# A delta-rule attention with a two-layer network behind it: 17 wide weight parts, a first inverse on blocks of 16, 64-column key products, beta in one load

## The chip, the core and the metric

The program runs on one core of a Trainium2 chip. A core has TensorE (PE, matrix products into PSUM), VectorE (DVE), ScalarE (ACT), GpSimd (POOL), and SyncE (SP), which here issues all DMAs. Each engine has its own stream of instructions and waits on semaphores. The metric is device microseconds of one execution, lower is better; the time before is the median of three runs.

## What is computed

For 4 x 8 heads of 768 tokens and 48 dimensions a state S (48 x 48) is carried along the tokens; its reads y, all heads side by side, are the rows of a two-layer network with relu squared.

```python
k_n = k / (np.linalg.norm(k, axis=-1, keepdims=True) + 1e-06)
for t in range(S):
    kt, vt, bt = (k_n[:, :, t], v[:, :, t], beta[:, :, t, None])
    y[:, :, t] = np.einsum('bhd,bhde->bhe', q[:, :, t], state)
    v_old = np.einsum('bhde,bhd->bhe', state, kt)
    state = state + bt[..., None] * np.einsum('bhd,bhe->bhde', kt, vt - v_old)
x = y.transpose(0, 2, 1, 3).reshape(B * S, H * D)      # 3072 x 384
out = np.maximum(x @ w_in, 0.0) ** 2 @ w_out           # 384 x 2048, 2048 x 384
```

q, k, v and beta are float32, the two weight matrices are float64.

## The kernel before

**Tiling.** The 768 tokens are 12 units of 64 (C); two units are a pair. Within a unit the recurrence is a triangular system: with L the strictly lower part of the scaled k k^T, T is the inverse of I + L, and w = T (v - k S). L is cut into 32 x 32 blocks (HB). All heads go through DVE at once: partitions hold the head and a row, the free dimension holds columns.

**What a unit needs.** `load_blocks` brings k or q as 32 x 32 blocks into one of two staging buffers kb, 8 DMAs on SP each, and `turned` (L246) transposes them with one DVE instruction into kt or qt; the first ones go through TensorE (`turned_by_pe`, L240, copied by ACT in L243). `load_v` and `load_rows` bring v and a second copy of k (kpad).
- `key_products`, once per pair: 32 x 32 products of kt with itself, for each of 32 heads and two units two diagonal blocks (L266) and one low block (L270), 192 in all; ACT copies the low part to mt.
- `prepare`: norms and beta (bt, 16 DMAs a pair in `load_beta`), lt = scaled L.
- `invert`: 31 steps of two DVE operations on all 32 x 32 blocks of the pair (L312 a product into tmp, L314 a subtraction from z). `ended` scales z and turns it twice (L319, L322 zt, L324 t).
- `below`, per unit: the off-diagonal block of T by two passes of products (L332, L333, then L343, L344) with ACT copies into tt.
- `query_products`: q k^T (L357), masked by DVE into ap (L361).
- `state_part`: k S (L387), subtracted from vt by DVE (L389); q S (L396), T times the rest (L402), copied to w; the state (L412) and y (L418).

**The network, `moe(u)`.** TensorE turns y (L431, three transposes for each of two token halves); ACT and DVE split it into a high and a low fp32r half, x_h (L433) and x_l (L434). For eight column pairs: up products L464 (three terms by three row parts, twice: 18 products), relu (L471), square (L472), cast h_h (L474) on ACT, the low half h_l (L443) on DVE, later 12 down products L451 into two PSUM tiles o. L486 copies the result, L491 writes it.

**The weights** come in 28 parts (128 x 512 of w_in, 128 x 384 of w_out) as pairs of 32-bit words. `split_weights` makes two fp32r halves of each part: `least` (Abs on ACT L125, a maximum on POOL L126), `words` (DVE L133, L136, L139, L140; a cast on ACT L143), `low` (three products on TensorE L149, a copy on ACT L150). Parts use two rooms (tiles a and rest; r and h_l) up to part 10 and one room after it.

**Order.** TensorE, SP, DVE and ACT run in the order in which the code is written (`tc.manual_schedule`); POOL's is left to a scheduler. `weave` lays generators against the 34 steps of `moe(u - 1)`, each step at a position in the stage, given in fractions:

```python
parts.append((loads(u), [0.02, 0.2, 0.3, 0.57, 0.62, 0.78, 0.85, 0.96], True))
parts.append((key_products(nxt), [0.18], False))           # odd u
parts.append((inverse, spread(0.34, 1, F1), True))         # odd u, F1 = 21
parts.append((inverse, spread(0, 0.26, HB - 1 - F1), True))  # even u
parts.append((splits, spread(0, 0.88, NW - 6), False))     # u = 1
```

A stage u is thus the attention of unit u with the network of unit u - 1. Odd stages hold the key products of the next pair, its preparation and 21 inversion steps; even stages the other ten, `ended`, and `below` for both units. Before stage 1 stands the start: unit 0's attention, with the first weight parts split between. Where a generator asks for a weight that isn't split, `half_of` drives the split on at that place.

Of the kernel before, what the change touches and what calls it, by code (L numbers as in the profile page):

```python
# [20 lines left out]
def kernel(  # L21
# [13 lines left out]

    nc = tc.nc
    B, H, S, D = q.shape
    DM, DF = w_in.shape
    P = 128
    C = 64  # L40
    HB = 32
    NP = H // 2
# [4 lines left out]
    units = S // C  # L47

    turn = [0, 0]
    const = ctx.enter_context(tc.tile_pool(name="const", bufs=1))  # L50
    wpool = ctx.enter_context(tc.tile_pool(name="weights", bufs=1))
    apool = ctx.enter_context(tc.tile_pool(name="attn", bufs=2))
# [5 lines left out]

    warm = const.tile([P, 1], F32, name="warm")
# [3 lines left out]
    kb = []  # L63
    for i in range(2):
        t = const.tile([P, 2 * X, C], F32, name=f"kb{i}")
        nc.gpsimd.memset(t[:, :, D:], 0.0)
        kb.append(t)
    plus, minus = [const.tile([P, P], F32R, name=n) for n in ("plus", "minus")]
    eye = spool.tile([P, 512], F32, name="a")[:, :P]
    make_identity(nc, eye)  # L70
    nc.scalar.copy(out=plus, in_=eye)
    nc.scalar.mul(out=minus, in_=eye, mul=-1.0)
    ident = plus.bitcast(F32)

    mask = const.tile([P, C], F32, name="mask")
    nc.gpsimd.memset(mask, 1.0)
    for b in range(2):
        half = mask[b * C:(b + 1) * C]
        nc.gpsimd.affine_select(out=half, in_=half, pattern=[[1, C]], base=0, channel_multiplier=-1,
                                compare_op=ALU.is_gt, fill=0.0)  # L80
    kp = const.tile([P, 2, X, C], F32, name="kpad")
    nc.gpsimd.memset(kp[:, :, :, D:], 0.0)
    ttile = []
    for i in range(2):
        tt = const.tile([P, 2, X, C], F32, name=f"tt{i}")
        nc.gpsimd.memset(tt[:, :, :, :HB], 0.0)
        ttile.append(tt)
# [3 lines left out]
    PC = 512  # L91
    EACH = PC // P
    weight_parts = []
    for part in range(DF // PC):
        weight_parts += [("wi", (kt, part), w_in[kt * P:(kt + 1) * P, part * PC:(part + 1) * PC]) for kt in range(KT)]
        weight_parts += [("wo", ft, w_out[ft * P:(ft + 1) * P]) for ft in range(part * EACH, (part + 1) * EACH)]
    NW = len(weight_parts)
    place = [f"w{x}" for x in range(NW)]
    raws = []
    halves = {}  # L100

    rooms = [(spool, "a", "rest"), (mpool, "r", "h_l")]
    AHEAD = 10

    def fetch(n):
        for _ in range(n):
            x = len(raws)
            if x < NW:
                src = weight_parts[x][2]
                raw = wpool.tile([P, src.shape[1], 2], I32, name=place[x])  # L110
                nc.sync.dma_start(out=raw.rearrange("p a b -> p (a b)"), in_=src.bitcast(I32))
                raws.append(raw)

    def room(x, n):
        pool, first, second = rooms[x % 2 if x < AHEAD else 0]
        return pool.tile([P, PC], I32, name=first)[:, :n], pool.tile([P, PC], I32, name=second)[:, :n]

    def split_weights():


        def least(x):

            w1 = raws[x][:, :, 1]
            a, rest = room(x, w1.shape[1])
            nc.scalar.activation(out=a.bitcast(F32), in_=w1.bitcast(F32), func=AF.Abs)  # L125
            nc.gpsimd.tensor_scalar(out=a.bitcast(F32), in0=a.bitcast(F32), scalar1=LEAST, scalar2=None, op0=ALU.max)  # L126
            return x, a, rest

        def words(x, a, rest):
            raw = raws[x]  # L130
            w1 = raw[:, :, 1]

            nc.vector.tensor_scalar(out=a, in0=a, scalar1=3, scalar2=0x3FFFFFF8,  # L133
                                    op0=ALU.logical_shift_left, op1=ALU.bitwise_and)

            nc.vector.scalar_tensor_tensor(out=a, in0=w1, scalar=-0x40000000, in1=a,  # L136
                                           op0=ALU.bitwise_and, op1=ALU.bitwise_or)

            nc.vector.tensor_scalar(out=w1, in0=a, scalar1=-0x800000, scalar2=None, op0=ALU.bitwise_and)  # L139
            nc.vector.scalar_tensor_tensor(out=rest.bitcast(F32R), in0=raw[:, :, 0].bitcast(U32), scalar=2.0 ** -52,  # L140
                                           in1=w1.bitcast(F32), op0=ALU.mult, op1=ALU.mult)
            hl = wpool.tile([P, 2, raw.shape[1]], F32R, name=place[x])
            nc.scalar.copy(out=hl[:, 0], in_=a.bitcast(F32))  # L143
            return x, a, rest, hl

        def low(x, a, rest, hl, bank):
            ps = bank()[:, :hl.shape[2]]
            for n, (m, y) in enumerate(((ident, a.bitcast(F32)), (minus, hl[:, 0]), (plus, rest.bitcast(F32R)))):
                nc.tensor.matmul(ps, lhsT=m, rhs=y, start=(n == 0), stop=(n == 2))  # L149
# [508 lines left out]
```

## Time and profile before

| | us |
|---|---|
| median of three runs | 794.68 (790.76 to 798.01) |
| the profiled execution, own time | 788.97 |
| its span in the profile | 787.3 |
| TensorE busy | 644.2 (82%) |
| VectorE busy | 381.9 (49%) |
| ScalarE busy | 313.0 (40%) |
| GpSimd busy | 53.8 (7%) |
| weights landed | about 62 |

The profiled execution lies 0.7% under the median. A row of the profile names a line, an engine, an operation, the tile written and the tiles read; "<-" in brackets behind it names what ended the wait ahead of it. A product of f32 operands shows as two TensorE records, so 64 such products are 128 records. The granted clock is a share of TensorE's full speed. Shares over the whole span mix the start, stage 1 and the later stages, which the prediction takes apart.

### The profile page before, as it was taken

What the parts mean: (1) busy time and instruction counts of PE and PEld (TensorE: products, weight loads), DVE (VectorE), ACT (ScalarE), POOL (GpSimd) and SP (SyncE); (2) the same over time, 40 slices, a digit from 0 to 9 for tenths busy, and PEclk for the clock granted to TensorE, in tenths of its full rate; (3) what the DMA queues carried; (4) which work ended last, traced back from release to release, by engine and by line L of the source; (5) the groups of instructions that cost most, each with busy time, mean ns of one, the idle gap of its engine ahead of it and who ended that gap; (6) DMA issues with size and microseconds to landing.
All of it is one profiled execution on the core that took longest, in us unless ns stands there. A gap on an engine that the chain in (4) does not pass through costs nothing.

```text
span 787.3 us, 25119 instructions
## 1 busy us (share of the span) xinstructions
PE 644.2 (82%) x11368; PEld 592.5 (75%) x11368; DVE 381.9 (49%) x777; ACT 313.0 (40%) x544; POOL 53.8 (7%) x55
## 2 busy tenths in 40 slices
PE   4407757575788979979979889798898998899997
PEld 3304635363587979979979879798798998799997
DVE  0597533645484225871337833178623577232121
ACT  2215533343334524334533445243544343445443
POOL 2203111222101000001000010000100000000000
PEclk9999777987898988998989989899999899899999
DMA  7993200010132311313212323114132023110000
GB/s 144 191 397 100 38 2 2 1 21 0 22 41 43 59 28 22 50 15 62 42 24 43 41 44 62 23 22 62 25 55 49 4 50 53 22 24 22 1 20 21
DMA packets 152939, 38.30 MB, mean 49 GB/s; under 512 B 146176, under 2 KB 149248, under 8 KB 152832
## 3 DMA queue, kind: packets, MB, share of 16 engines
q1 hardware_dynamic: 152832, 36.69, 23.3%
q8 instruction: 89, 1.46, 0.8%
q14 instruction: 18, 0.15, 0.1%
HBM read 31.95 MB, written 4.72 MB: 47 GB/s over the span
## 4 chain that ended last, share of the span: by engine, by line
PE 65%; DVE 18%; issue 6%; ACT 3%; SPq 2%; DMA 2%; POOL 1%; DVEq 0%; POOLq 0%
PE h L464 25%; PE o L451 23%; DVE tmp L312 3%; DVE z L314 3%; PE g L149 2%; PE g L266 2%; PE g L387 2%; PE g L357 2%; PE g L402 1%; DVE zt L322 1%; PE g L412 1%; PE g L418 1%; DVE h_l L443 1%; DVE rest L140 1%; PE g L396 1%
## 5 line engine op out<-in xcount | busy, mean ns | idle before, releaser
L451 PE MATMUL o<-w,h_h 128*128 128x384 f32 x768 | 209.2, 354 | 0.0
L464 PE MATMUL h<-x_h,w 128*128 128x256 f32 x1152 | 186.4, 300 | 24.3 <-DVE x_l L434 12.6
L443 DVE TENSOR_TENSOR h_l<-r,h_h 128x512 fp32r<-128x512 f32 x96 | 66.0, 688 | 258.1 <-PE o L451 163.2
L464 PEld LDWEIGHTS h<-x_h,w 128*128 128x128 f32 x1152 | 166.6, 204 | 29.7 <-issue 15.4
L451 PEld LDWEIGHTS o<-w,h_h 128*128 128x128 f32 x768 | 139.8, 197 | 2.4
L451 PE MATMUL o<-w,h_l 128*128 128x384 f32 x384 | 133.5, 348 | 0.0
L471 ACT ACTIVATE r<-h 128x512 f32<-128x512 f32 x96 | 57.4, 598 | 177.9 <-PE h L464 173.0
L464 PE MATMUL h<-x_l,w 128*128 128x256 f32 x576 | 105.8, 295 | 0.3
L464 PEld LDWEIGHTS h<-x_l,w 128*128 128x128 f32 x576 | 88.1, 203 | 0.9 <-DVE x_l L434 0.9
L451 PEld LDWEIGHTS o<-w,h_l 128*128 128x128 f32 x384 | 75.5, 197 | 0.0
L314 DVE TENSOR_TENSOR z<-z,tmp 128x31 f32<-128x31 f32 (+15 forms) x186 | 64.0, 344 | 6.4
L312 DVE TENSOR_TENSOR tmp<-lt,z 128x31 f32<-128x31 f32 (+15 forms) x186 | 62.6, 337 | 4.2 <-DVE lt L302 0.5
L472 ACT ACTIVATE r<-r 128x512 f32<-128x512 f32 x96 | 60.7, 632 | 3.1
L474 ACT CAST h_h<-r 128x512 fp32r<-128x512 f32 x96 | 59.6, 621 | 3.0
L143 ACT CAST w<-a 128x384 fp32r<-128x384 f32 (+1 forms) x23 | 12.7, 553 | 86.8 <-DVE rest L140 86.8
L149 PE MATMUL g<-a,plus 128*128 128x384 f32 (+1 forms) x42 | 24.6, 674 | 21.5 <-ACT w L150 16.2
L266 PE MATMUL g<-kt 48*32 48x32 f32 x1536 | 25.8, 225 | 15.3 <-issue 15.3
L126 POOL TENSOR_SCALAR a<-a 128x384 f32<-128x384 f32 (+1 forms) x23 | 29.7, 1292 | 112.9 <-ACT a L125 89.0
L266 PEld LDWEIGHTS g<-kt 48*32 48x32 f32 x1536 | 23.5, 124 | 17.2 <-issue 16.6
L332 PE MATMUL g<-zt,mt 32*32 32x32 f32 x384 | 11.9, 211 | 27.5 <-DVE zt L322 27.5
L270 PE MATMUL g<-kt 48*32 48x32 f32 x768 | 24.8, 223 | 10.1 <-issue 9.2
L332 PEld LDWEIGHTS g<-zt,mt 32*32 32x32 f32 x384 | 9.8, 122 | 29.7 <-issue 18.8
(109 smaller groups left out, 710.0 us busy)
## 6 DMA issues: line engine op xcount, KB each, us to landing
w<-in_moe_w_in_dram SPq DMA_DIRECT2D x12, 512.0 KB
w<-in_moe_w_out_dram SPq DMA_DIRECT2D x16, 384.0 KB
vt<-in_v_dram SPq DMA_DIRECT2D x48, 96.0 KB
kpad<-in_k_dram SPq DMA_DIRECT2D x48, 96.0 KB
out_dram<-a SPq DMA_DIRECT2D x48, 96.0 KB
kb<-in_q_dram SPq DMA_DIRECT2D x44, 64.0 KB
kb<-in_k_dram SPq DMA_DIRECT2D x32, 64.0 KB
kb<-in_k_dram SPq DMA_DIRECT2D x8, 192.0 KB
```

Of the source, the lines that this page charges most:

```text
L126: nc.gpsimd.tensor_scalar(out=a.bitcast(F32), in0=a.bitcast(F32), scalar1=LEAST, scalar2=None, op0=ALU.max)
L149: nc.tensor.matmul(ps, lhsT=m, rhs=y, start=(n == 0), stop=(n == 2))
L266: nc.tensor.matmul(d["diag"][(up, lo)[s](b), j, at], lhsT=half, rhs=half, start=True, stop=True)
L270: nc.tensor.matmul(low[(lo, up)[j](b), at], lhsT=first, rhs=second, start=True, stop=True)
L312: nc.vector.tensor_tensor(out=tmp, op=ALU.mult, in0=lt[:, s:s + 1, s + 1:].broadcast_to([P, nj, nt]), in1=z[:, :nj, s:s + 1].broadcast_to( ...
L314: nc.vector.tensor_tensor(out=z[:, :nj, s + 1:], in0=z[:, :nj, s + 1:], in1=tmp, op=ALU.subtract)
L443: nc.vector.tensor_tensor(out=h_l, in0=r, in1=h_h.bitcast(F32), op=ALU.subtract)
L451: nc.tensor.matmul(o[i], lhsT=a[:, e, i * P:(i + 1) * P], rhs=half_of(("wo", ft))[w], start=(ft == 0 and n == 0), stop=(ft == FT - 1 and n ...
L464: nc.tensor.matmul(hp[:, e], lhsT=half_of(("wi", (kt, ft // EACH)))[w][:, f], rhs=x[:, kt], start=(n == 0), stop=(n == 3 * KT - 1))
L471: nc.scalar.activation(out=r, in_=hp, func=AF.Relu)
L472: nc.scalar.activation(out=r, in_=r, func=AF.Square)
L474: nc.scalar.copy(out=h_h, in_=r)
```

## The change

- **Weights.** 17 parts: w_in in nine of 768, 768 and 512 columns, w_out as eight, each two row blocks side by side (128 x 2 x 384). The tile a has three buffers; Abs and maximum of part x + 2 are issued behind part x's words; a part's DVE operations are four separate steps; the three products of `low` are made for two halves of columns, six matmuls into a two-bank tile. Twelve parts are split in the start, at places given by a list (`fill`), five in stage 1.
- **Beta** is loaded once, 4 DMAs, and spread to the partitions of all six pairs by four products with a shifted identity (eye).
- **Key products** are made per unit: one product of 64 columns for each 32 key rows (128 a pair in place of 192 of 32 columns). ACT copies the diagonal part (dg), and with it a masked part (goff) for pairs 0 and 1.
- **Inverse.** For pairs 0 and 1 (FAST = 2) the DVE steps run on two 16 x 16 blocks of each 32 x 32 block: 15 steps instead of 31. `corrected` adds what is missing: 64 products, an ACT copy, 128 products, and two DVE subtractions for each unit. From pair 2 on there are 31 steps as before, 23 of them in the odd stage.
- **Buffers.** One staging tile kb in place of two (kb1, kb2, kb3 of the start lie in tiles ap and tt); qt, vt, ap, w and y have one buffer; tt is one tile for both units and the second transpose writes into it; h_l has three buffers; both network sums o are one tile; for units 0 and 1 the mask of ap is made by an ACT copy and POOL.
- **Places.** A table A gives the position of each piece; `need` states what must stand ahead of it.

```diff
-    PC = 512
+    PC = 768
...
+        for ft in range(a // P, b // P, 2):
+            src = w_out[ft * P:(ft + 2) * P].rearrange("(f p) n -> p f n", f=2)
+            weight_parts.append((("wo", ft // 2), src, 2, DM))
...
+            a = spool.tile([P, PC], I32, name="a", bufs=3)[:, :n]
             nc.scalar.activation(out=a.bitcast(F32), in_=w1.bitcast(F32), func=AF.Abs)
             nc.gpsimd.tensor_scalar(out=a.bitcast(F32), in0=a.bitcast(F32), scalar1=LEAST, scalar2=None, op0=ALU.max)
...
+            for c in range(2):
+                for m, (i, z) in enumerate(terms):
+                    nc.tensor.matmul(ps[:, c], lhsT=i, rhs=z.rearrange("p (c n) -> p c n", c=2)[:, c],
+                                     start=(m == 0), stop=(m == len(terms) - 1))
+            nc.scalar.copy(out=hl[:, 1].rearrange("p (c n) -> p c n", c=2), in_=ps)
...
+            before = x, a, rest, hl
+            if x + 2 < NW:
+                ready[x + 2] = least(x + 2)
+            yield
...
+                nc.tensor.matmul(global_ps.rearrange("p (d t) -> p d t", t=HB), lhsT=eye[:, off:off + P].bitcast(F32),
+                                 rhs=by[:, i, s], start=(n == 0), stop=(n == 3))
...
-                            nc.tensor.matmul(d["diag"][(up, lo)[s](b), j, at], lhsT=half, rhs=half, start=True, stop=True)
...
-                        nc.tensor.matmul(low[(lo, up)[j](b), at], lhsT=first, rhs=second, start=True, stop=True)
...
+                        key = kt[dims(j), b * X + x]
+                        both = key.rearrange("p (s t) -> p s t", s=2)
+                        nc.tensor.matmul(g[(up, lo)[s](b), j, :, x], lhsT=both[:, s], rhs=both[:, ::-1] if s else both,
+                                         start=True, stop=True)
...
+        if d["pair"] < FAST:
...
+            for s in range(QB - 1):
+                nj, nt = s + 1, QB - 1 - s
+                tmp = tmp_[:, :2 * nj * nt].rearrange("p (h j t) -> p h j t", h=2, t=nt)
...
+    def corrected(d, i):
...
+                    nc.tensor.matmul(ps[r, j, 0, x], lhsT=goff[r, j, i, x], rhs=t1[r, j, i, x], start=True, stop=True)
...
+                    nc.tensor.matmul(ps[r, j, 0, x], lhsT=yt[r, j, x], rhs=z[r, j, x], start=True, stop=True)
+                    nc.tensor.matmul(ps[r, j, 1, x], lhsT=z[r, j, x], rhs=yt[r, j, x], start=True, stop=True)
...
+        nc.vector.tensor_tensor(out=z[:, :, :, QB:], in0=z[:, :, :, QB:], in1=ps[:, :, 0, :, QB:], op=ALU.subtract)
+        nc.vector.tensor_tensor(out=t1[:, :, i, :, :QB], in0=t1[:, :, i, :, :QB], in1=ps[:, :, 1, :, :QB], op=ALU.subtract)
...
-            h_l = mpool.tile([P, 2, 2 * P], F32R, name="h_l", bufs=2)
+            h_l = mpool.tile([P, 2, 2 * P], F32R, name="h_l", bufs=3)
...
+                    parts.append((key_products(nxt, 0), at["kk0"], False))
+                    parts.append((key_products(nxt, 1), at["kk1"], False))
...
+                    parts.append((inverse, spread(*at["inverse"], A["first"] if u > 1 else QB - 1), True))
```

**TensorE, start of an odd stage (u = 3).** L431/L628 turn y, L464/L664 are up products, L451/L648 down products, L266, L270/L363 key products. Before:

```order
L431 MATMUL h<-plus,y 128x128 x3
L451 MATMUL o_2159<-w_2013,h_h 128x384 x2
L451 MATMUL o_2159<-w_2013,h_l 128x384
...
L387 MATMUL g<-state,kt 64x48 x32
...
L464 MATMUL h<-x_l,w_614 128x256
L464 MATMUL h<-x_l,w_663 128x256
L464 MATMUL h<-x_l,w_713 128x256
L266 MATMUL g<-kt 32x32 x8
L270 MATMUL g<-kt 32x32 x4
```

After:

```order
L648 MATMUL o<-w_1810,h_h 128x384 x2
L648 MATMUL o<-w_1810,h_l 128x384
L628 MATMUL h<-eye,y 128x128 x3
L363 MATMUL g<-kt 32x2x32 x64
L664 MATMUL h<-x_h,w_362 128x256
...
L664 MATMUL h<-x_l,w_510 128x256
L363 MATMUL g<-kt 32x2x32 x64
L664 MATMUL h<-x_h,w_362 128x256
```

The two last rows of before come sixteen times in one run; after, one half of the key products stands behind the turned y and the other a good way into the stage, with up products around both.

**DVE, start of an even stage (u = 4).** L246/L340 turns the queries, L434/L631 makes x_l, L312, L314/L446, L448 are the inversion, L372/L562 scales v. Before:

```order
L246 STREAM_TRANSPOSE qt<-kb_82 128x1024
...
L372 TENSOR_TENSOR vt<-vt,nr 128x768
...
L312 TENSOR_TENSOR tmp<-lt,z 128x207
L314 TENSOR_TENSOR z<-z,tmp 128x23x9
L434 TENSOR_TENSOR x_l<-h,x_h 128x3x128
L312 TENSOR_TENSOR tmp<-lt,z 128x192
L314 TENSOR_TENSOR z<-z,tmp 128x24x8
```

After:

```order
L562 TENSOR_TENSOR vt<-vt,nr 128x768
L446 TENSOR_TENSOR tmp<-lt,z 128x207
L448 TENSOR_TENSOR z<-z,tmp 128x23x9
L639 TENSOR_TENSOR h_l<-r,h_h 128x512
L340 STREAM_TRANSPOSE qt<-kb 128x1024
L631 TENSOR_TENSOR x_l<-h,x_h 128x3x128
L446 TENSOR_TENSOR tmp<-lt,z 128x192
L448 TENSOR_TENSOR z<-z,tmp 128x24x8
```

Before, seven inversion steps stand between the turned queries and the first x_l; after, none does, and the turning stands at the stage's start.

**DVE, the start of the program.** L133 to L140 and L239 to L249 are a weight part's words. Before:

```order
L314 TENSOR_TENSOR z<-z,tmp 128x31
L319 TENSOR_TENSOR z<-z,bt 128x1024
L322 STREAM_TRANSPOSE zt<-z 128x32x32
L324 STREAM_TRANSPOSE t_607<-z 128x32x32
L133 TENSOR_SCALAR a<-a 128x512
L136 SCALAR_TENSOR_TENSOR a<-w_130,a 128x512
```

After:

```order
L435 TENSOR_TENSOR tmp<-t_401,z 128x78
L437 TENSOR_TENSOR z<-z,tmp 128x2x3x13
L249 SCALAR_TENSOR_TENSOR rest<-w_135 128x768
L435 TENSOR_TENSOR tmp<-t_401,z 128x96
L437 TENSOR_TENSOR z<-z,tmp 128x2x4x12
L239 TENSOR_SCALAR a<-a 128x768
L242 SCALAR_TENSOR_TENSOR a<-w_137,a 128x768
```

The inversion before ran to its end and its transposes before the next part's words; after, the words of several parts stand between its steps.

More of the change, by code (lines that the diff above doesn't have):

```diff
@@ L41 @@
     HB = 32
+    QB = 16
     NP = H // 2
@@ L143, in words @@
             nc.scalar.copy(out=hl[:, 0], in_=a.bitcast(F32))
[L144 to L149, printed above, removed]
-            nc.scalar.copy(out=hl[:, 1], in_=ps)
-            halves[weight_parts[x][:2]] = hl[:, 0], hl[:, 1]
-        before, ready = None, []
@@ L309, in invert @@
+        tmp_ = apool.tile([P, 256], F32, name="tmp")
         for s in range(HB - 1):
@@ L592 @@
-        for _ in state_part(0):
-            take(splits, 1)
+        step()
+        step(key_products(pairs[0], 0))
+        step(key_products(pairs[0], 1))
+        first = prepare(pairs[0])
+        for _ in range(8):
+            step(first)
+        turned_by_pe(kb2, new_qt(0))
+        turned_by_pe(kb3, new_kt(2))
+        nc.gpsimd.memset(tt[:, :, :, :, 0], 0.0)
+        inverse = invert(pairs[0])
+        for n in range(QB - 1):
+            step(inverse)
+            if n == 3:
+                step(query_products(0))
+                turned_by_pe(kb, new_qt(1))
@@ L594 @@
+        step(scale_v(0, pairs[0]))
+        for gen, n in ((ended(pairs[0]), 4), (corrected(pairs[0], 0), 3), (below(pairs[0], 0), 2), (state_part(0), 2)):
+            for _ in range(n):
+                step(gen)
         load_v(1)
         load_rows(kp, k, 1, True)
-        load_beta(pairs[1])
-        take(scale_v(1, pairs[0]))
         split_early = False
@@ L601 @@
             pair, nxt = pairs[u // 2], pairs[(u + 1) // 2] if u + 2 < units else None
+            at = {**A["odd" if u % 2 else "even"], **A.get(u, {})}
             parts, s = [], state_part(u)
             if before:
-                parts += [(before, spread(0, E2, OVER + 1), False), (before, [0.22], True)]
+                parts += [(before, spread(0, at["end"], at["over"] + 1), False), (before, [at["out"]], True)]
+            more = u + 1 < units
             if u == 1:
-                parts.append((splits, spread(0, 0.88, NW - 6), False))
@@ L607 @@
-                parts.append((below(pair, 1), [0.06, 0.12], False))
-            parts.append((loads(u), [0.02, 0.2, 0.3, 0.57, 0.62, 0.78, 0.85, 0.96], True))
+                parts.append((splits, spread(*at["splits"], 4 * NW + 2), False))
+                parts.append((corrected(pair, 1), at["corrected1"], False))
+                parts.append((below(pair, 1), at["below1"], False))
+                parts.append((iter(scale_v(1, pairs[0])), at["v1"], True))
+            parts.append((s, at["state"], False))
@@ L624 @@
             before = moe(u - 1)
-            weave((before, n_moe - OVER, M0, M1), parts)
+            weave((before, n_moe - A["odd"]["over"], at["m0"], at["m1"]), parts)
         take(before)
```

532 lines of the change are left out of this document (345 added, 187 removed).

## The prediction

> **What bounds the kernel now.** I read the table of stretches first, cut where the transposes of a unit's y start on TensorE (L431; its program order has them once per unit), because one share over the whole span mixes three different limits.
>
> ```profile
> span 787.3 us, 25119 instructions
> core 0: us, PE busy (x) PEld busy (x) DVE busy (x) ACT busy (x) POOL busy (x), PEclk, DMA share, GB/s
> 0.00:80.08 80.08, 34.15 (x836) 25.10 (x837) 45.63 (x102) 22.73 (x44) 17.41 (x26) 1.00 0.75 206
> 80.08:223.90 143.82, 97.92 (x1223) 75.70 (x1222) 73.98 (x157) 54.16 (x105) 27.48 (x21) 0.80 0.07 12
> 223.90:277.32 53.42, 48.12 (x887) 45.24 (x886) 26.83 (x48) 25.56 (x43) 2.22 (x2) 0.94 0.33 50
> 330.34:386.06 55.72, 49.84 (x887) 46.86 (x886) 27.38 (x49) 25.55 (x43) 2.22 (x2) 0.91 0.32 49
> 386.06:437.74 51.68, 47.20 (x1015) 45.92 (x1014) 27.68 (x65) 18.51 (x31) 0.00 (x0) 0.93 0.15 29
> 437.74:703.86 266.12, 240.84 (x4688) 230.18 (x4687) 135.46 (x271) 113.67 (x191) 4.43 (x4) 0.93 0.24 39
> 703.86:746.53 42.67, 42.67 (x579) 41.84 (x578) 9.54 (x15) 17.99 (x30) 0.00 (x0) 1.00 0.05 11
> 748.27:787.30 39.03, 34.13 (x240) 33.81 (x240) 6.42 (x10) 15.31 (x25) 0.00 (x0) 1.00 0.08 19
> ```
>
> A start of 80 us; a unit 1 of 143.8 us in which TensorE is busy two thirds; then stages of 51 to 56 us, TensorE-bound but for small holes. The stage 703.86 to 746.53 has no hole and the full clock: the yardstick of what a stage costs when nothing waits. The last 40.8 us are two-layer work alone.
>
> Next, what holds unit 1: the timeline of DVE, ACT and POOL for one 512-column weight part.
>
> ```profile
> 139.08 0.43 DVE L133 TENSOR_SCALAR a<-a 128x512 int32<-128x512 int32 x1 [0.51 <-POOL a L126]
> 140.87 0.69 DVE L140 SCALAR_TENSOR_TENSOR rest<-w 128x512 fp32r<-128x512 uint32 x1
> 141.60 0.62 ACT L143 CAST w<-a 128x512 fp32r<-128x512 f32 x1 [4.12 <-DVE rest L140]
> 142.49 0.68 ACT L125 ACTIVATE a<-w 128x512 f32<-128x512 f32 x1
> 143.25 1.49 POOL L126 TENSOR_SCALAR a<-a 128x512 f32<-128x512 f32 x1 [4.20 <-ACT a L125]
> 144.77 0.43 DVE L133 TENSOR_SCALAR a<-a 128x512 int32<-128x512 int32 x1 [2.07 <-POOL a L126]
> PE g L149 <- ACT w L150: 18.5, 7, 4.3
> ```
>
> It is a ring: DVE's words, ACT's cast and Abs, POOL's maximum, DVE again, 5.69 us a part with no engine full, since the Abs of the next part is issued only behind this part's cast. TensorE waits at the end of the ring (last row, from the list of waits).
>
> Third, the holes of the even and odd stages, from the timeline and the chain of waits, and what the clock does behind them.
>
> ```profile
> 335.71 0.47 PE L464 MATMUL h<-x_h,w 128*128 128x256 f32 x2 [2.45 <-DVE x_l L434]
> 352.86 0.24 PE L332 MATMUL g<-zt,mt 32*32 32x32 f32 x2 [1.84 <-DVE zt L322]
> 354.62 0.25 PE L333 MATMUL g<-t,mt 32*32 32x32 f32 x1 [1.51 <-DVE t L324]
> 395.61 2.65 issue
> 399.87 1.84 issue
> 354.00:361.00 7.00, 6.38 (x140) 5.84 (x141) 1.25 (x2) 2.84 (x6) 2.22 (x2) 0.52 0.63 108
> 361.00:398.00 37.00, 34.61 (x863) 33.15 (x863) 10.12 (x13) 17.06 (x29) 0.00 (x0) 1.00 0.25 40
> 355.69 4.14 PE o L451 x12
> 369.62 2.08 PE o L451 x12
> 402.15 4.71 PE h L464 x27
> ```
>
> An even stage idles 5.8 us for DVE, an odd one 4.5 us inside the key products. Behind each hole the granted clock is 0.5 for 3.4 to 7 us and twelve products of L451 take 4.14 us, not 2.08: a hole costs about half as much again.
>
> **The change, part by part.** *Key products.* 384 matmul records a pair (192 f32 products) become 256 (128 products of 64 columns), in two batches of 128 records with L464 work between.
>
> ```profile
> 393.47:402.15 8.68, 4.20 (x386) 0.77 0.22 50
> 390.05:391.12 1.07, 1.07 (x65) 1.00 0.00 0
> 379.23:379.91 0.68, 0.68 (x65) 1.00 0.07 12
> ```
>
> These rows of stretches, for PE alone, are the key products (386 records, 4.20 us busy in 8.68), a state product (48 columns on 64-wide weights, 16.5 ns a record) and a product of below (10.5 ns). The new record lies between 10.9 and 16.5 ns; nearer the first, as its weights are 32 wide, so 13.5 ns: 3.5 us (2.8 to 4.2). The two stalls stand 128 records apart, and the first comes some 190 small records into a burst; a batch of 128 with slow L464 and L451 products ahead of it stays under that. I take both stalls as gone, with the slow clock behind them (27 products of L464 take 4.71 us there against 3.2, so 1.5 us). The Trainium skill's page "Runtime: NRT & Kernel Launch", section "Instruction fetch mechanics", says that instructions come in blocks of 256 and that the crossing of a block is mostly hidden; 128 records with their weight loads are such a block, so the spacing agrees, but the rows show 2.65 and 1.84 us, not hidden. By the page this part would save nothing, and the time would come out 25 us higher.
>
> *Stages from unit 3 on.* The yardstick of 42.67 us lacks a state update (1.07) and holds twelve more L451 products than other stages (2.08): 41.66 us. Odd: plus 3.5 and a switch of 0.2, and 0.4 for what remains, 45.8 (51.68 before). Even: plus four passes of below at 0.9 each with the switches, 45.3; DVE's chain there I follow below; 46.0 (55.72 before).
>
> In an even stage DVE reached x_l behind fourteen inversion operations. Now 23 instead of 21 inversion steps stand in the odd stage, all ahead of its last eighth, so x_l follows turnings at once; and the products of below stand 4.8 us of TensorE work later (18+18+18+12+18+12 products ahead, not 18+36+6+18) while DVE has two steps less. By the old row widths DVE ends its second transpose 18.2 us into the stage, TensorE is there at 17.6: 0.7 us of wait, for 3.35. A third h_l buffer takes away DVE's waits on L451. Single buffers for kb, qt, tt and ap put a load behind the transpose that frees it; on SP that load is followed by no one earlier than before.
>
> ```profile
> 356.17 4.37 SPq L217 DMA_DIRECT2D kb<-in_q_dram  x8
> 436.75 2.12 DMA kb<-in_k_dram
> ```
>
> One reload is 4.4 us of issue on SP and 2.1 us to land, 6.5 us; in the even stage it starts with the turning of qt, 0.8 us in, and DVE asks for it at 8.9. Covered by 1.6 us; should that cover go, DVE is late there, and below behind it.
>
> *Inverse on blocks of 16.* For pairs 0 and 1, 62 operations become 30.
>
> ```profile
> 29.38 0.19 DVE L312 TENSOR_TENSOR tmp<-lt,z 128x31 f32<-128x31 f32 x1
> 45.49 0.42 DVE L312 TENSOR_TENSOR tmp<-lt,z 128x256 f32<-128x256 f32 x1
> 57.39 0.21 DVE L314 TENSOR_TENSOR z<-z,tmp 128x31 f32<-128x31 f32 x1
> 40.15 0.95 DVE L372 TENSOR_TENSOR vt<-vt,nr 128x768 f32<-128x768 f32 x1
> 58.90 1.97 DVE L322 STREAM_TRANSPOSE zt<-z 128x1024 f32<-128x1024 f32 x1
> 10.34 1.07 ACT L243 COPY kt<-g 128x512 f32<-128x512 f32 x2 [1.25 <-PE g L240]
> ```
>
> 0.16 us and 1.0 ns an element: 30 operations on 2,720 elements with their gaps, 8.4 us, where the old stretch from 29.38 to 57.6 was 28.2. The correction costs 192 products, 384 records, for each unit: 4.05 us at below's 10.5 ns. It comes four times: once in the start, once in unit 1, twice in unit 2, which goes to 45.3 + 8.1 + 1.4 of switches + 1.5 of waits = 56.3 (53.4 before). DVE's saving there hides under TensorE.
>
> *Start, and where the weights go.* Twelve of 17 parts are now split in the start, not 7 of 28. Beta in 4 DMAs frees SP early, and weights are fetched sooner; no DVE row waits for them in this count. First words: the key copies end at 11.4, Abs 0.9 and a maximum of 2.1 (1.49 at 512) lead to 15.0. To the second transpose and two parts on, DVE has seven parts at 3.1 us (two operations like L372's 0.95, two of about 0.6), 21.7; the inverse 8.4; preparation 5.4; scaling and endings 1.9; two transposes 3.9: 41.3, with 4 us of waits on the key products 60. The correction's results come at 66.5, as part 5 (two triples of products) lies between its halves on TensorE and its cast waits for DVE. Then five parts go through in turn with below, state and y.
>
> ```profile
> 94.49 1.02 PE g L149 x4
> 123.44 2.07 PE g L149 x4
> ```
>
> A triple of 384 columns is 1.02 us at the full clock and 2.07 at half; a part is two, with ACT's copy of 0.8 that the next must wait for: 2.8 to 5 us, 4.3 taken, 21.5 for five. So y is turned at 88 (82 with DVE's words alone, 95 with the slow clock throughout): later than the old 80.
>
> *Unit 1.* Of the work left: 41.66, key products 3.7, below 1.8, correction 4.75, six parts' products 11.6 (three at 512): 63.5. To it two fetch stalls of 2.4, 1.3 us where y's chain stands at the end without filler, and 3.4 for the clock behind such holes: 73 (66 to 85), for 143.8. The ring does not bind: Abs runs two parts ahead with three rooms, 7.3 us for two parts, and only five parts remain.
>
> *Sum.* 88 + 73 + 56.3 + 4 x 45.8 + 4 x 46.0 + 42.7 + 40.8 = 668.0; with 1.7 around the span (788.97 against 787.3) 669.7 us, 15.1% under the profiled 788.97. The median of the runs, 794.68, lies 0.7% above the profiled one; on it the forecast is 674.
>
> **Rivals.**
> - *The ring still sets unit 1.* ACT and POOL each serve more columns a part; were every remaining part to pass at the old 5.69 us scaled to 768 (8.5) with TensorE waiting, five parts add about 27 us: 703. The rows that speak for it are those of the ring; against it, the earlier Abs.
> - *The even stages' waits only move.* If DVE is as late as before (x_l or the transposes, with the clock), four even stages stay near 55: 36 us more, 711. For it: 18.2 against 17.6 above.
> - *A floor under small products.* Were each small record to start 25 ns after the last, 256 key records would take 6.4 us and a correction 9.6: 2.9 us in five odd stages, 5.5 in four corrections, 36 us more, 711. The Trainium skill's page "TensorE: Matmul & The Clock Gate", section "Wait — 56ns, not 53.3ns?", states such a floor of about 25 ns. The rows show 10.5 to 16.5 ns, so it gets little chance.
> - *Slower: one staging buffer.* Every k and q block now passes kb. If each of 19 turnings from unit 2 on waits out a whole reload, 6.5 us and 1.7 of slow clock behind it, 156 us come back: 830. It decides from 6.3 us a turning, and the even stage's cover is thin, but the odd one's k load starts 9 us ahead.
>
> **How the numbers follow.** Forecast 0.62; ring 0.12; waits moved 0.14; floor 0.05; staging 0.02; the rest, two at once, 0.05. The forecast's own bounds, 82 + 66 + 501 and 95 + 85 + 525, are 656 and 712 on the median's scale; the three middling rivals end at 711. I take 650 to 714, which leaves out about 0.15. All but the staging case are over 1% faster (about what this kernel's measurement can tell from no change): faster 0.97, same 0.01, slower 0.02.
>
> **What would show it.** Right: y first turned at 82 to 95; the second turn 66 to 85 later; odd stages near 46 with no issue hole over 1 us in the key products; even ones near 46 with DVE waits under 1.5 us; the granted clock near 1.00 from unit 3 on; unit 2 longer than its neighbours. Wrong: TensorE waiting on ACT's L223 copy through unit 1 (ring), on x_l or the transposes in even stages (moved waits), on kb's DMA (staging), or key products above 4.2 us a pair (floor).

## The result, and where the time went

| | us |
|---|---|
| before, median of four runs | 793.87 (790.76 to 798.01) |
| changed, median of four runs | 663.44 (663.01 to 666.5) |
| changed to before | 0.8363 (95% interval 0.8316 to 0.8409) |
| forecast | 674 (650 to 714) |
| changed, the profiled execution and its span | 663.01, 661.3 |

The changed kernel is 16.4% faster, and the time lies in the forecast's range, 1.6% under the forecast of 674. The table of stretches of the changed kernel, cut as before where the first transposes of a unit's y start on TensorE (L628 now); the columns are length, busy time of each engine with its instructions, granted clock, DMA share and GB/s:

```profile
span 661.3 us, 26439 instructions
0.00:86.48 86.48, 59.38 (x1160) 42.74 (x1161) 59.27 (x97) 42.99 (x65) 42.11 (x48) 0.82 0.63 187
86.48:149.54 63.06, 60.04 (x1435) 54.58 (x1435) 34.32 (x66) 36.04 (x59) 13.73 (x10) 1.00 0.16 24
149.54:215.98 66.44, 58.23 (x1655) 53.76 (x1654) 25.38 (x44) 24.17 (x41) 0.00 (x0) 0.95 0.28 45
215.98:260.86 44.88, 44.88 (x888) 43.33 (x887) 35.11 (x75) 19.97 (x34) 2.22 (x2) 1.00 0.24 39
260.86:305.96 45.10, 45.10 (x887) 43.22 (x886) 22.33 (x38) 23.11 (x39) 0.00 (x0) 1.00 0.35 55
486.42:531.98 45.56, 45.00 (x887) 43.28 (x886) 35.25 (x75) 20.07 (x34) 2.22 (x2) 1.00 0.21 37
577.09:619.81 42.72, 42.72 (x580) 41.65 (x578) 9.37 (x14) 17.87 (x29) 0.00 (x0) 1.00 0.05 11
```

Against the forecast's terms, all on the scale of the span:

| stretch | before | forecast | measured | off by |
|---|---|---|---|---|
| start, to the first turned y | 80.1 | 88 | 86.5 | -1.5 |
| stage 1 | 143.8 | 73 | 63.1 | -9.9 |
| stage 2 | 53.4 | 56.3 | 66.4 | +10.1 |
| stages 3, 5, 7, 9 together | 207.2 | 183.2 | 180.7 | -2.5 |
| stages 4, 6, 8, 10 together | 219.3 | 184.0 | 180.4 | -3.6 |
| stage 11 | 42.7 | 42.7 | 42.7 | 0 |
| the last network | 40.8 | 40.8 | 41.5 | +0.7 |

From stage 3 on TensorE is full but for one wait of 0.6 us in stage 9, and its clock 1.00: an even stage is 45.1 us, busy 45.10. The two stages ahead of them hold two errors of ten microseconds that cancel; without either one the time would still have been in the range, but not so near the forecast. (The start's clock of 1.00 in the table of before is no measure against the 0.82 here: that trace has no clock record ahead of 70.5 us, and the kernel before with the Abs drawn ahead, whose start is as long, shows 0.64.) Stage 2 has waits for x_l and waits for which the profile shows no releaser ("issue"); here are the longest rows of its list of waits on TensorE (total, times, longest), the only row of that list for stages 3 to 10, and after it rows of stretches, TensorE alone, for the two corrections in it (three pieces of 64 products each) and for one half of the key products in stage 3:

```profile
PE h L664 <- DVE x_l L631: 4.5, 1, 4.5
PE g L496 <- issue: 1.9, 2, 1.2
PE g L486 <- issue: 1.5, 2, 0.8
PE g L363 <- issue: 0.6, 1, 0.6
166.61:168.82 2.21, 1.43 (x130) 1.00 0.40 60
171.15:172.98 1.83, 1.57 (x129) 1.00 0.41 38
174.22:176.56 2.34, 1.64 (x130) 1.00 0.00 0
198.84:200.99 2.15, 1.42 (x130) 1.00 0.45 81
202.26:205.05 2.79, 1.55 (x130) 1.00 0.00 0
206.89:208.82 1.93, 1.93 (x130) 0.50 0.00 0
217.79:219.20 1.41, 1.41 (x129) 1.00 0.05 12
```

The six pieces take 13.25 us where 8.1 were forecast: each holds a stall without a releaser or runs at the clock of 0.50 behind one. This half of the key products, of the same length, takes 1.41 us, 11 ns a record.

What these stalls are, the traces can tell. The page counts the packets of a queue that carries instructions, 16 KB each (packets, MB, share of 16 engines):

```profile
q8 instruction: 95, 1.56, 1.0%
```

TensorE's program has 24,401 instructions, weight loads counted, so 95 full blocks of 256 (the kernel before has 22,807 and 89 packets: 89 blocks). Counted in TensorE's own order, 128 of the 129 stalls of over 0.2 us without a releaser in the fourteen traces stand at the 194th to 196th instruction of such a block, and each of them ends 1.2 to 1.6 us after the latest of these packets has landed. So TensorE waits there for its next block. 128 small records with their weight loads are a whole block. The five stalled blocks of stage 2 lasted 2.7 to 3.7 us without their stall and 3.5 to 4.0 with it: a block used up sooner than the next arrives has to wait, and the six to fifteen large products between two pieces of one correction were too few to fill that time; ahead of its first piece stand other small products. Of the three pieces of unit 1's correction in stage 1 the second, nine up products behind the first, stalls 0.7 us; the third, behind 27, does not stall.

The x_l of unit 1 comes 4.5 us late, and the 18 up products behind it take 3.62 us, not the 2.15 of a later stage (chain of waits):

```profile
156.99 3.62 PE h L664 x18
...
274.90 2.15 PE h L664 x18
```

An even stage (45.1), the corrections (13.25), the wait (4.5) and the slow clock behind it (1.5) make 64.4. Of the other 2 us, 0.6 are nine up products at the slow clock behind the longest of the corrections' stalls (1.91 us for 1.34); the rest, about the 1.4 that the forecast had for switches between small and large products, was not taken apart.

### The profile page after: what moved, and what is told of

Its sections match the earlier page's. It is cut to its first block, busy times and chain, and to the rows that moved or that the text cites. A ratio compares the mean times of both kernels' runs of the same rounds, so it can differ in the third digit from the quotient of the medians.

```text
span 661.3 us, 26439 instructions
## 1 busy us (share of the span) xinstructions
PE 615.6 (93%) x12160; PEld 573.3 (87%) x12160; DVE 364.8 (55%) x678; ACT 310.1 (47%) x514; POOL 64.7 (10%) x65
## 4 chain that ended last, share of the span: by engine, by line
PE 84%; DVE 8%; issue 3%; ACT 2%; DMA 1%; SPq 1%; DVEq 0%; ACTq 0%
PE h L664 33%; PE o L648 30%; PE g L363 3%; PE g L579 2%; PE g L537 2%; PE g L589 2%; PE g L595 2%; DVE tmp L435 1%; PE g L607 1%; PE g L613 1%; PE g L495 1%; DVE z L437 1%; PE o L221 1%; DVE a L242 1%; PE g L221 1%
## 5 line engine op out<-in xcount | busy, mean ns | idle before, releaser
L648 PE MATMUL o<-w,h_h 128*128 128x384 f32 x768 | 199.4, 340 | 0.0
L664 PE MATMUL h<-x_h,w 128*128 128x256 f32 x1152 | 176.3, 289 | 5.7 <-DVE x_l L631 5.7
L664 PEld LDWEIGHTS h<-x_h,w 128*128 128x128 f32 x1152 | 153.5, 191 | 10.2 <-issue 4.8
L648 PEld LDWEIGHTS o<-w,h_h 128*128 128x128 f32 x768 | 133.5, 188 | 0.9
L648 PE MATMUL o<-w,h_l 128*128 128x384 f32 x384 | 128.9, 336 | 0.0
L664 PE MATMUL h<-x_l,w 128*128 128x256 f32 x576 | 101.2, 285 | 0.0
L664 PEld LDWEIGHTS h<-x_l,w 128*128 128x128 f32 x576 | 83.6, 193 | 0.2 <-DVE x_l L631 0.2
L648 PEld LDWEIGHTS o<-w,h_l 128*128 128x128 f32 x384 | 72.1, 188 | 0.0
L674 ACT CAST h_h<-r 128x512 fp32r<-128x512 f32 x96 | 59.6, 621 | 3.0
L448 DVE TENSOR_TENSOR z<-z,tmp 128x31 f32<-128x31 f32 (+15 forms) x124 | 42.5, 343 | 4.2
L206 POOL TENSOR_SCALAR a<-a 128x768 f32<-128x768 f32 (+1 forms) x17 | 37.9, 2234 | 59.5 <-ACT a L205 58.7
L446 DVE TENSOR_TENSOR tmp<-lt,z 128x31 f32<-128x31 f32 (+15 forms) x124 | 42.1, 340 | 2.8
L221 PE MATMUL o<-a,eye 128*128 128x384 f32 x44 | 24.9, 656 | 5.8 <-DVE a L242 4.1
L631 DVE TENSOR_TENSOR x_l<-h,x_h 128x384 fp32r<-128x384 f32 x24 | 13.1, 554 | 22.0 <-ACT x_h L630 22.0
L363 PE MATMUL g<-kt 48*32 48x64 f32 x1536 | 19.4, 234 | 5.9 <-issue 5.7
L363 PEld LDWEIGHTS g<-kt 48*32 48x32 f32 x1536 | 16.9, 109 | 8.5 <-issue 7.7
L630 ACT CAST x_h<-h 128x384 fp32r<-128x384 f32 x24 | 11.3, 480 | 27.3 <-PE h L628 27.3
```

Source lines behind the costliest of these rows:

```text
L221: nc.tensor.matmul(ps[:, c], lhsT=i, rhs=z.rearrange("p (c n) -> p c n", c=2)[:, c], start=(m == 0), stop=(m == len(terms) - 1))
L363: nc.tensor.matmul(g[(up, lo)[s](b), j, :, x], lhsT=both[:, s], rhs=both[:, ::-1] if s else both, start=True, stop=True)
L446: nc.vector.tensor_tensor(out=tmp, op=ALU.mult, in0=lt[:, s:s + 1, s + 1:].broadcast_to([P, nj, nt]), in1=z[:, :nj, s:s + 1].broadcast_to( ...
L448: nc.vector.tensor_tensor(out=z[:, :nj, s + 1:], in0=z[:, :nj, s + 1:], in1=tmp, op=ALU.subtract)
L648: nc.tensor.matmul(o[:, i, :DM], lhsT=a[:, e, i * P:(i + 1) * P], rhs=w_[w], start=(ft == 0 and n == 0), stop=(ft == FT - 1 and n == 2))
L664: nc.tensor.matmul(hp[:, e], lhsT=half_of(("wi", kt, part))[w][:, f], rhs=x[:, kt], start=(n == 0), stop=(n == 3 * KT - 1))
```

## The experiments

Each is cut at the same transposes, and its span stands against the changed kernel's 661.3 us. All but the last ran once. The stages from 3 on, where an edit doesn't touch them, repeat within 0.8 us; the span of the changed kernel itself was 661.3 to 664.8 us in its four runs, so differences of a few microseconds are read from stages and not from spans.

**Both halves of the key products in one run.**

```diff
-                    parts.append((key_products(nxt, 0), at["kk0"], False))
-                    parts.append((key_products(nxt, 1), at["kk1"], False))
+                    parts.append((both_products(nxt), at["kk1"], False))
...
```

> Changed kernel with both halves of a pair's key products at the second half's place, 256 records in one run. Prediction's theory: the stall comes with the length of a run of small products, so each odd stage from 3 on gets one issue stall of 2 to 2.7 us and 1 to 1.5 us of slow clock behind it: 48 to 49.5 us a stage for 45.1, span 673 to 680. Rival: it was the number of products, 384 records for 256, and their place doesn't matter: 45.1 to 45.6 a stage, span 661 to 664.

The chain of waits of this kernel in stage 7, and the stretches of stages 3, 4 and 7:

```profile
415.66 1.15 PE g L363 x75
416.81 0.54 issue
417.35 1.50 PE g L363 x86
418.85 2.54 issue
421.38 0.66 PE g L363 x26
422.04 5.74 PE h L669 x27
219.78:268.60 48.82, 46.39 (x887) 44.73 (x886) 33.82 (x74) 20.17 (x34) 2.22 (x2) 0.97 0.22 37
268.60:313.71 45.11, 45.11 (x887) 43.23 (x886) 23.52 (x39) 23.12 (x39) 0.00 (x0) 1.00 0.35 55
408.22:458.68 50.46, 47.38 (x888) 45.70 (x887) 34.74 (x75) 20.18 (x34) 2.22 (x2) 0.93 0.19 34
```

Two stalls are back, 128 records apart, 0.54 and 2.54 us, and 27 up products behind the second take 5.74 us (18 take 2.15 at the full clock, so 27 take 3.2). The four odd stages are 48.8 to 50.5 us, together 18.4 more than in the changed kernel; two of them, and the span of 683.4 (stages 1 and 2 grow by 1.8 and 2.6), lie above the theory's range. The number of products is the same as in the changed kernel, so it isn't that which stalls: a run of 256 records holds a whole block of nothing but small products. The even stages don't move.

**Unit 0's key products ahead of unit 1's turning**, so that the start has no run of 256 either.

```diff
+        done.add(("keys", 0))
+        take(key_products(pairs[0], 0))
         load_plain(kb, q, 1)
         turned_by_pe(kb1, new_kt(1))
...
-        step(key_products(pairs[0], 0))
+        step()
```

> Changed kernel with unit 0's key products ahead of unit 1's turning, in place of both units' in one run of 256 records. Theory: the first half runs while k of unit 1 is still landing, neither half is long enough to stall, and the 5.2 us issue stall of the start goes: first y turned 4 to 7 us earlier, at 80 to 82, span 654 to 657. Rival: DVE's words and inversion bind the start anyway, or the stall moves to another place of fresh code: first y at 85 to 87, span 659 to 662.

The first y is turned at 86.29, the span is 661.9: the rival. The stall did go, 5.2 us to 1.0, but TensorE then waits longer for the words. The lists of waits, of the changed kernel's start and of this one's:

```profile
PE g L363 <- issue: 5.2, 1, 5.2
PE o L221 <- DVE a L242: 4.1, 1, 4.1
...
PE o L221 <- DVE a L242: 7.8, 2, 4.7
PE g L363 <- issue: 1.0, 1, 1.0
```

**Nine weight parts in the start in place of twelve.**

```diff
-     'fill': [2, 1, 1, 1, 0, 1, 0, 1, 0, 0, 0, 0, 0, 1, 0, 3, 0, 1, 0, 0, 1, 0, 0, 2, 0, 0, 1, 2, 1, 1, 2, 2, 4, 0, 4, 4, 4,
-              4, 4],
+     'fill': [2, 1, 1, 1, 0, 1, 0, 1, 0, 0, 0, 0, 0, 1, 0, 3, 0, 1, 0, 0, 1, 0, 0, 2, 0, 0, 1, 2, 1, 1, 2, 2, 4, 0, 0, 4, 0,
+              4, 0],
```

> Changed kernel with nine weight parts split in the start in place of twelve; the other three go to stage 1. Theory: a part costs the start about 4 us (words on DVE, two copies on ACT, the triples between the halves of a chain) and stage 1 only its 1.94 us of products, since no ring binds there: first y at 74 to 78, stage 1 at 67 to 70, span 653 to 659. Rival (ring in stage 1): each moved part costs stage 1 5.7 us or more, 80 or more, span 664 or more.

Both theories fall in part. The start is no shorter, 87.6, and stage 1 is 11.7 us longer, 74.7, so 3.9 us a part; the span is 675.0. Rows of stretches, TensorE's L221 alone, behind pair 0's inversion, first in the changed kernel (six parts), then in this one (three):

```profile
58.60:86.48 27.88, 15.38 (x48) 0.88 0.13 25
...
57.50:87.59 30.09, 12.30 (x24) 0.67 0.10 20
```

With three parts less between the short steps of the chain the granted clock falls from 0.88 to 0.67, and a part's products take 4.1 us where they took 2.6: 4.6 us for the three that stay. TensorE's waits without a releaser in this stretch grow as well, from 1.8 to 4.9 us; one of them, of 2.0 us, is the only one of the 129 that stands at no block's end, and its cause is open. The words there filled holes; taking them out gave the time back as slow clock and stalls.

**The kernel before with the Abs two parts ahead**, and a third buffer for a and rest; nothing else of the change.

```diff
-    spool = ctx.enter_context(tc.tile_pool(name="staging", bufs=2))
+    spool = ctx.enter_context(tc.tile_pool(name="staging", bufs=3))
...
-            far = 3 if x < AHEAD - 3 else 1
+            far = 3 if x < AHEAD - 3 else 2
```

> The kernel before with a third buffer for the tiles a and rest and the Abs and maximum always two parts ahead; nothing else. Theory: the ring through this part's cast and the next part's Abs held stage 1 at 5.7 us a part; without it the stage falls from 143.8 towards TensorE's own 98, to 100 to 115, and the span from 787 to 745 to 762. Rival: the ring is only one of several couplings of the same strength (in-order DVE, h_l, the places in the weave): stage 1 at 130 or more, span 770 or more.

```profile
80.14:200.21 120.07, 88.13 (x1224) 70.45 (x1222) 75.28 (x157) 54.78 (x105) 29.01 (x21) 0.84 0.09 15
PE g L149 <- ACT w L150: 16.3, 7, 4.2
```

Stage 1 falls by 23.7 us, to 120.1; the rest of the span hardly moves (763.5). The ring was real and worth 23.7 of the 80.8 us that stage 1 lost in the change, between the two expectations. Of these 80.8 us, 37.9 are TensorE's busy time (97.9 before, 60.0 after): the products of six wide parts run there in place of those of 23 narrower ones, and the clock is 1.00 in place of 0.80; 42.9 are idle time. With the Abs two parts ahead alone, the idle time falls by 14.0 and the busy time by 9.8. TensorE still waits 16.3 us for ACT's copy of the low half, almost as before (18.5): that wait is the turn from one part's products to the next. In stage 1 of the changed kernel, with six parts' products left there, no wait for that copy is listed; how much of the rest is due to that was not tried by itself.

**DVE's order at the start of the even stages, put back in part.**

```diff
-              'inverse': [0.02, 0.2509],
+              'inverse': [0.0, 0.2509],
...
-             'inverse': [0.333, 0.863],
+             'inverse': [0.333, 1.0],
...
-             'queries': [0.5821, 0.9082],
+             'queries': [0.5821, 0.96],
```

> Changed kernel with DVE's order at the start of the even stages put back part of the way: the 23 inversion steps of an odd stage reach to its end, the queries are turned at 0.96, and two steps stand between that and x_l. Theory of the prediction: x_l then comes late behind inversion steps, 1.5 to 2.5 us of wait and 1 to 2 us of slow clock in each even stage from 4 on: 47.5 to 49 for 45.1, span 671 to 677. Rival: DVE has enough slack in the odd stages (35 us busy in 45) that the order doesn't matter: 45.1 to 45.6, span 661 to 664.

```profile
258.58:305.08 46.50, 45.35 (x887) 43.17 (x886) 24.64 (x43) 23.12 (x39) 0.00 (x0) 1.00 0.35 53
```

Each even stage from 4 on costs 1.4 us more, 46.5, between both expectations. The hole at x_l is there (1.1 us), but the clock stays at 1.00 behind it. (Only part of the old order was put back; the places of the products of below weren't tried apart.) The span rises by less than these four stages, to 663.9, since the start and stage 2 came out 0.9 and 1.3 us shorter.

**Two buffers for h_l in place of three** (`bufs=3` to `bufs=2`).

> Changed kernel with two buffers for h_l in place of three. Theory of the prediction: the third buffer takes away DVE's waits on L451 (the down products), and without it DVE reaches x_l and the transposes late: even stages 46.5 to 49, span 667 to 677. Rival: those waits lie in DVE's spare time at the new places: all stages within 0.3 us, span 661 to 664.

The rival from stage 3 on: DVE's waits on the down products are back, but no stage there is over 0.3 us longer. Stage 2 misses the rival's 0.3: it takes 67.9 us, where it takes 66.4 to 66.6 in the three runs that leave it alone, and its x_l comes 5.6 us late in place of 4.5. The span is 663.1. The group of h_l, of the changed kernel and of this one (busy, mean ns, idle before it and what ended that), and this kernel's wait in stage 2:

```profile
L639 DVE TENSOR_TENSOR h_l<-r,h_h 128x512 fp32r<-128x512 f32 x96 | 65.6, 686 | 162.2 <-ACT h_h L674 162.0
L639 DVE TENSOR_TENSOR h_l<-r,h_h 128x512 fp32r<-128x512 f32 x96 | 65.7, 687 | 177.6 <-PE o L648 98.4 <-ACT h_h L674 43.5 <-ACT tt L523 26.7
PE h L664 <- DVE x_l L631: 5.6, 1, 5.6
```

**What pair 1's 16-blocks are worth.** First they are left out for pair 1. Its inversion then has 31 steps, 23 of them in stage 1, and stage 2 takes the places of the other even stages:

```diff
-    FAST = 2
+    FAST = 1
...
-            at = {**A["odd" if u % 2 else "even"], **A.get(u, {})}
+            at = {**A["odd" if u % 2 else "even"], **(A.get(u, {}) if u // 2 < FAST or u == 1 else {})}
...
-                if u > 2:
+                if u // 2 >= FAST:
...
```

> Changed kernel with the 16-blocks for pair 0 alone; pair 1 gets the full inversion, 31 steps, 23 of them in stage 1, and no correction in stage 2. Theory: the two corrections hold TensorE for about 13 us of stage 2's 66.4 (fetch stalls included), and the sixteen DVE steps more delay x_l there by about 5 us: stage 2 about 58, span about 652. Rival: DVE is what binds around the start of stage 2, and 62 inversion operations in place of 30 cost there what the corrections cost TensorE: stage 2 at 66 or more, span 661 or more.

Stage 2 is 61.4 (5.0 less), between the two expectations, the span 656.5. The corrections' 13 us are gone, but x_l is now 14.8 us late:

```profile
150.09:211.51 61.42, 46.67 (x887) 44.49 (x886) 38.04 (x74) 23.12 (x39) 0.00 (x0) 0.89 0.30 48
PE h L664 <- DVE x_l L631: 14.8, 1, 14.8
```

Then the places of the remaining split steps, alone and together with the first edit:

```diff
-         'splits': [0.0083, 0.8254],
+         'splits': [0.0083, 0.6],
...
-                parts.append((splits, spread(*at["splits"], 4 * NW + 2), False))
+                parts.append((splits, spread(*at["splits"], 21), False))
```

> Changed kernel with the 21 split steps that remain for stage 1 spread over 0.01 to 0.60 of it, in place of 70 places of which only the first 21 hold work. Theory: stage 1's network steps were drawn ahead of the attention, so pair 1's key products and inversion ended late and DVE reached stage 2's x_l 4.5 us late; spread evenly, the key products come about half way, the hole goes with the slow clock behind it: stage 2 about 60, stage 1 62 to 65, span about 656. Rival: the hole comes from the number of DVE operations in the two stages, not from when the key products come: stage 2 stays at 66, or what it gains stage 1 loses, span 660 to 664.

> Both edits together: 16-blocks for pair 0 alone and the 21 split steps spread evenly. Theory: with the key products early, DVE has the room in stage 1 for 23 full steps, and stage 2 is an even stage like the others: 45 to 49, span 640 to 646. Rival (DVE binds around stage 2's start): stage 2 at 55 or more, span 650 or more.

Alone, stage 2 is 62.3 (x_l waits 2.1) and stage 1 grows to 65.3; the span is 660.2, in the rival's range. Together, stage 1 is 68.8 and stage 2 52.6, the span 655.7: much less than the theory's gain, with stage 2 between the two expectations. Spread evenly, the words stand between the steps of DVE's inversion, and that still ran behind unit 1's y (5.6 us of wait for x_l).

Next, the first edit with most of pair 1's inversion placed behind x_l:

```diff
+     2: {'inverse': [0.03, 0.42],
+         'below0': [0.52, 0.56],
+         'state': [0.13, 0.6, 0.77],
...
+         'ended': [0.43, 0.45, 0.46, 0.48]},
...
+    FAST = 1
+    EARLY = 8
...
```

> Changed kernel, 16-blocks for pair 0 alone; pair 1's full inversion has 8 steps in stage 1 and 23 in stage 2, these behind x_l and spread to 0.42 of the stage, its transposes at 0.43 to 0.48, the products of below for unit 2 at 0.52 and 0.56. Theory: fast1's stage 2 lost 14.8 us waiting for x_l behind inversion steps, and about 2 of slow clock; with x_l ahead of them nothing waits: stage 1 as before, 62 to 63, stage 2 46 to 49, span 641 to 645. Rival: the wait moves on to the transposes of pair 1, since DVE has some 30 us of work ahead of them: stage 2 at 53 or more, span 648 or more.

The rival again, in size: stage 2 is 59.6, the span 653.0. x_l waits 1.8 us, but the wait has moved on to the transposes, 6.3 and 1.5 us. So pair 1's key products were drawn ahead, with 18 steps in stage 1, and stage 2's places moved with them:

```diff
-         'kk1': [0.24],
-         'prepare': [0.2358, 0.4],
+         'kk1': [0.18],
+         'prepare': [0.181, 0.29],
...
-         'inverse': [0.43, 0.8747],
+         'inverse': [0.3, 0.71],
...
+     2: {'inverse': [0.03, 0.33],
+         'below0': [0.46, 0.52],
...
+         'ended': [0.34, 0.36, 0.38, 0.4]},
...
+    EARLY = 18
```

> As late_inverse (16-blocks for pair 0 alone), but with pair 1's second half of key products and its preparation drawn ahead in stage 1, right behind the products of below, and 18 inversion steps in stage 1 behind them, 13 in stage 2 behind x_l. Theory: the waits of stage 2 came from where pair 1's key products stand (134 us, 15 us before the stage's end); some 12 us earlier, DVE has done 18 steps before unit 1's y, and neither x_l nor the transposes are late by over 1.5 us: stage 1 62 to 65, stage 2 45 to 49, span 640 to 646. Rival: in stage 1 DVE and ACT have no room, since the words of five parts and h_l stand in the same order; the work only lengthens stage 1 as in fast1_even21: stages 1 and 2 together over 116, span over 650.

```profile
PE h L666 <- DVE x_l L633: 6.4, 1, 6.4
PE g L512 <- DVE tt L473: 1.7, 1, 1.7
126.27 2.05 DVE L382 STREAM_TRANSPOSE lt<-z 128x1024 f32<-128x1024 f32 x1 [1.80 <-ACT z L370]
139.86 0.18 DVE L448 TENSOR_TENSOR tmp<-lt,z 128x31 f32<-128x31 f32 x1
158.22 0.98 DVE L633 TENSOR_TENSOR x_l<-h,x_h 128x384 fp32r<-128x384 f32 x2
```

Stage 1 is 63.4 and stage 2 59.0, together over the rival's 116, though stage 1 is hardly longer. The place of the key products was not what bound. DVE turns them at 126.3 where the changed kernel does at 136.3, ten microseconds earlier, but starts the inversion at 139.9, only three earlier than there (143.2): the last words and h_l stand between the steps of the preparation. The span is 654.6. The last kernel keeps this and moves eight steps behind x_l, the queries' turning ahead of the state update, unit 2's products of below to 0.67, and with them the places of the transposes, the state and v in stage 2:

```diff
+         'queries': [0.5821, 0.705],
...
+     2: {'inverse': [0.03, 0.5],
+         'below0': [0.67, 0.715],
+         'below1': [0.91, 0.965],
+         'values': [0.7676, 0.88, 0.9476],
+         'state': [0.13, 0.755, 0.87],
...
+         'ended': [0.52, 0.54, 0.56, 0.58]},
...
+    EARLY = 10
```

> As keys_early (16-blocks for pair 0 alone, pair 1's key products and preparation early in stage 1), but with 10 inversion steps of pair 1 in stage 1 and 21 in stage 2, the queries of unit 2 turned ahead of the state update, pair 1's transposes at 0.52 to 0.58 of stage 2 and the first products of below at 0.67 and 0.715. Theory: keys_early's x_l came 6.4 us late behind eight inversion steps of 0.85 us; with these behind x_l it comes in time, and DVE has its transposes done some 30 us into stage 2, where TensorE now asks for them after 27 to 28: stage 1 63 to 64, stage 2 46 to 50, span 642 to 646, its own time 644 to 648. Rival: what is taken from one place of DVE's order in these two stages comes back at the other, as in late_inverse and keys_early: stages 1 and 2 together 121 to 123 again, span 652 to 656.

```profile
86.50:150.37 63.87, 60.60 (x1436) 54.72 (x1435) 37.86 (x71) 35.33 (x57) 13.13 (x9) 1.00 0.16 24
150.37:202.93 52.56, 47.50 (x888) 45.00 (x886) 33.04 (x65) 23.02 (x39) 0.00 (x0) 0.97 0.30 50
PE g L516 <- DVE tt L477: 2.7, 1, 2.7
PE g L517 <- DVE t L479: 1.5, 1, 1.5
PE h L670 <- DVE x_l L637: 0.8, 1, 0.8
```

650.35 us (648.88 to 651.74), 0.8219 of the kernel before (0.8179 to 0.8259), against 0.8363 (0.8316 to 0.8409) for the changed kernel: the intervals don't meet, so this version beats both. Stage 2 missed its expectation by 2.6 us (52.6 for 46 to 50), and the time by 2.4 (650.35 for 644 to 648), since the transposes are still 4.2 us late; stages 1 and 2 together are 116.4, against 129.5 in the changed kernel. So without pair 1's 16-blocks, and with places to suit, the kernel is 13 us faster by the medians, 11 by the two ratios. Pair 1's 16-blocks with better places were tried in one run alone, with the split steps spread evenly, so how much of this the places would have brought with them is open.

## Why the forecast held, point by point

- *Key products.* Right, and confirmed by putting them together again. The record costs 11 ns (1.41 us for 128), at the low end of the forecast's 10.9 to 16.5. The stalls are all but gone: from stage 3 on one of 0.56 us is left, in stage 9. The reason given, that a batch of 128 is short enough, was only half of it: what counts is how long a block of 256 instructions lasts, and the correction, in batches of 128 too, stalled. The 11 ns decide against the floor of 25 ns as well: the Trainium skill's page "TensorE: Matmul & The Clock Gate", section "Wait — 56ns, not 53.3ns?", has start to start never under about 25 ns, and these rows show less than half of it a record for products of 64 columns on 32-wide weights, which go to different parts of the array in turn. The Trainium skill's page "Runtime: NRT & Kernel Launch", section "Instruction fetch mechanics", has the crossing of a block mostly hidden: so it is here, for 86 of the changed kernel's 95 blocks, but nine cost 0.26 to 5.2 us each. What the forecast drew from the page, that this part would save nothing, did not come.
- *Even stages.* Right in result: 45.1 for 46.0, with no wait on DVE of a microsecond. Of the reasons, x_l's place was worth 1.4 us a stage by the part that was put back, and the step "a third h_l buffer takes away DVE's waits on L451" was true but worth nothing from stage 3 on, and 1.5 us in stage 2, by one run. By the rows of stage 4 (55.72 before, with 49.84 busy; 45.10 now, all busy), 5.9 of the 10.6 us were idle time and 4.7 the same 887 records at a granted clock of 0.91. What the places of below gave of it was not tried apart.
- *The ring.* It was read rightly as something that held unit 1, but not as all of it: alone it was worth 23.7 of 80.8 us, with fewer parts left there beside it. The rival that it still sets stage 1 did not come.
- *Start.* 86.5 for 88, with a step that doesn't hold: "4.3 taken, 21.5 for five" counted the parts behind the inversion as a sum of their own. A part's products there took 2.6 us, and with three parts fewer the start was as long. They fill the holes of the chain through correction, below and state, and hold the clock up.
- *Stage 1.* The work was 63.5 by the forecast and TensorE was busy 60.0; the terms "two fetch stalls of 2.4" and "3.4 for the clock behind such holes" came as one stall of 0.7 us, in the correction, and not at all. The split key products don't stall there, and the clock was 1.00. Like stage 2's error this was a miss; that the two are of one size is chance.
- *Stage 2.* Here the forecast failed, by 10.1 us, in two terms. "4.05 us at below's 10.5 ns" priced the correction by a row without a stall; it measured 6.4 and 6.9 us. And "DVE's saving there hides under TensorE", with 1.5 us of waits, took DVE to be in time: it ran 4.5 us behind x_l. The two errors have different roots. The first is the wait for the next block of instructions, which the forecast had seen in the key products and did not carry over to the correction. The second is DVE's order: stage 1 was taken as a place with room for pair 1's chain. DVE is busy there for only 34.3 of 63.1 us, but the chain starts late (its key products are turned at 136.3), and from 139.9 until x_l at 156.3 no wait of DVE is listed. The six experiments on it moved this wait about more than they removed it, whether the inversion was short or full.
- *One staging buffer.* In no run does TensorE wait for a transfer after the start; the longest wait of DVE for a staging load is 2.8 us, once, in the last kernel.

## What to carry to other kernels

A run of small products should be cut into pieces with enough large products between that each block of 256 TensorE instructions lasts as long as the next takes to arrive, here some 4 us; pieces of 128 records with little between them stalled too. A correction that replaces vector work by many small products must be priced with its stalls, not by the record alone. Work that filled the holes of the start's latency chain was free there, and taking three parts of it out cost as much in clock and stalls as it saved. When a stage loses a wait, follow the in-order engine to the next thing asked of it: moving pair 1's inversion turned a wait for x_l into one for the transposes and back, until both were paid in part.

## What was not expected of the hardware

- The length of a hole alone doesn't tell what follows: behind 4.5 us the 18 up products took 3.62 us, behind 2.54 us 27 took 5.74, and behind a stall of 1.24 us in stage 2 the clock was 0.50 for 3.4 us, but the 1.1 us of idle time in an even stage of the kernel with DVE's old order left it at 1.00.
- Where a run of 128 small records stalls is decided by where the blocks of 256 instructions end and what else stands in them. The second half of the key products passes without a stall in stage 3 and holds one of 0.56 us in stage 9, since the block's end moves by 16 records from one odd stage to the next. Of the nine pieces of the two pairs' corrections in stages 1 and 2 six stall, 0.3 to 1.2 us. No run moved the block ends alone, by padding; the account rests on their places and on the landing times of the packets.
